# A two-bank split, a shared last eviction and halved activation stores at the end of a fused attention and expert kernel

## The chip, the cores and the metric

The kernel runs on one core of a Trainium2 chip. The metric is device time in microseconds (us), one launch for the whole computation. Below, PE is the matrix engine, DVE the vector engine, ACT the scalar engine, POOL the GpSimd engine and SP the engine that issues nearly all transfers. ACTq and SPq are the instruction queues of ACT and SP, in which transfers are issued, semaphores awaited and branches taken.

## The reference

The inputs are q, k and v of shape (8 batches, 8 heads, 576 tokens, 64). Attention goes through 32 landmarks per head: `A = sm(q, k_lm)`, `Bm = sm(q_lm, k_lm)`, `C = sm(q_lm, k)`, where a landmark is the mean of 18 consecutive tokens, and `sm` is a softmax of the scaled products. `Z` is an approximate inverse of `Bm` after six steps of `Z = 2 Z - Z Bm Z`, and the output of attention is `A Z C v`, reshaped to 4608 rows of 512.

Each row is then given to one of eight experts, the one whose embedding has the largest cosine with it, and the result is

```
h = np.maximum(x[mask] @ w1[e], 0.0)
out[mask] = gate_w[mask, None] * (h @ w2[e])
```

with `w1[e]` 512 x 1024 and `w2[e]` 1024 x 512; the gate is the chosen expert's softmax probability. The output is 4608 x 512 in float32.

## The kernel before, in words

The kernel guesses one expert per batch from the batch's first results, runs all 576 rows of the batch through that expert, and counts the rows for which the guess was wrong. Only if that count is above zero does a general path run behind it: `general(...)` stands under `tc.If(left[0] > 0)` on L1590, and its code lies between that branch and the end of the program. With the given data the count is zero, so every engine branches over it, then waits at L1590 and L1630 for all work and ends.

Products are made in float16 with split operands: each operand is a high and a low part, and three products (high by high, high by low, low by high) are summed in PSUM. PSUM is one tile `ps` of eight banks of 512 float32 columns, and `take` hands out banks by number.

The instruction order is written out by hand. `Weave` runs generators, one for each piece of work, and the string `TURNS` says which generator goes next; `CHOICES` says which engine does a piece that either could do, and `BANKS` which bank a request gets. Each engine executes its instructions in the order in which they come out. The tile framework adds the semaphores: an instruction waits for the earlier ones that touch the same tile, and for `ps` the same bank. A transfer's issue may also be held until an older transfer has landed whose semaphore it reuses.

The pieces that the change touches:

- `held` (L957): the activations `ab[b]` of a batch, 128 partitions x 2 parts (high, low) x 2 x 576 in float16, are stored to DRAM (`abs_`, L967) for the general path, one transfer of 576 KB per batch on SP. There are three `ab` buffers for eight batches.
- `second` (L1478): the second product of a batch. For each group of 128 rows (`c` = 0 to 3; `c` = 4 is a group of 64 rows) eight weight pieces are multiplied into one bank `py`, three matmuls each. The very last group (batch 7, `c` = 3) is made in two halves of 256 columns: first all eight pieces for columns 0 to 255, then all eight for columns 256 to 511, both in the one bank of `py`. The matmuls are recorded on the helper's line L505.
- `outputs` (L1517): a finished group is multiplied by its gate factor on its way from PSUM to the SBUF tile `yt`, by DVE (L1533) or ACT (L1535), and stored by SP (L1540; the 64-row group by L1543). The last half goes to ACT alone, which also issues its store:

```
last = (b, c, cols.stop) == (B - 1, 3, DM)
...
(act if last else sp).dma_start(out[t0:t0 + P, cols], yt[:, 0:n])
```

Ahead of the eviction of the last group's first half, `values_load` (L1523) reads the count of wrong guesses into a register of every engine.

Two lines of `rows`, which the change leaves alone, matter to the prediction: on L1194 DVE sums the router columns (64 onward) of each half bank and on L1197 ACT squares the first 64 columns, so the two read different columns of the same banks, and write to different tiles.

Of the kernel before, what the change touches and what calls it, by code (L numbers as in the profile page):

```python
# [13 lines left out]
AF = mybir.ActivationFunctionType  # L14
ALU = mybir.AluOpType
# [4 lines left out]
P = 128  # L20
B, H, S, D = 8, 8, 576, 64
# [8 lines left out]
DM = H * D  # L30
# [115 lines left out]
def T(ns, n, lat=None, cols=None, tiles="whole"):  # L146

    return "use", "pe", ns, lat, (2.3 * ns if cols is None else cols, n), tiles
# [319 lines left out]
def nystrom_moe(ctx: ExitStack, tc: tile.TileContext, qT, kT, v, emb, w1, w2, out):  # L468
    nc = tc.nc
    vec, act, pool, pe, sp = nc.vector, nc.scalar, nc.gpsimd, nc.tensor, nc.sync  # L470
# [12 lines left out]
    def view(ids):  # L483

        return ps[:, ids[0]] if len(ids) == 1 else ps[:, ids[0]:ids[0] + len(ids)]

    def take(work, n, *shares):

        shares = shares or ("att",)
        if work:  # L490
            ids = yield (*work, n, shares)
        else:
            for x in shares:
                yield "get", x, None, n
            ids = yield "get", "bank", None, n

        def done():
            wv.put("bank", *ids)
            for x in shares:
                wv.put(x, *ids)  # L500

        return view(ids), done

    def mm(o, lhsT, rhs, start=True, stop=True):
        pe.matmul(o, lhsT, rhs, start=start, stop=stop)  # L505
# [74 lines left out]
    abs_ = dram.tile([B, P, 2, 2, S], F16, name="abs_")  # L580
    wgs_ = dram.tile([NU, P, 4, 2, WC], F16, name="wgs_")

    wv = Weave(bank=NBANKS - 1, att=99, quad=QUAD, ph=99, py=99, pv=99, half=1, **BUFS)
# [37 lines left out]
    qt, kt, vt, ab, abr, u0, x0, sums_of, rcs = {}, {}, {}, {}, {}, {}, {}, {}, {}  # L621
# [335 lines left out]
    def held(b):  # L957

        if b:
            yield "wait", ("ab", b - 1)  # L960
        i, = yield "get", "ab"
        abr[b] = abt[i]
        ab[b] = abt[i][:, PAD:PAD + 4 * S].rearrange("p (x g s) -> p x g s", x=2, g=2)
        wv.flag(("ab", b))
        yield "wait", ("rows", b)
        yield "use", "dma", TAKES["ab"], ISSUE["ab"]
        sp.dma_start(abs_[b], ab[b])  # L967
        yield "wait", ("first", b)
        wv.put("ab", i)

# [301 lines left out]
    def batch(b):  # L1272
        if b:
            yield "wait", ("begun", b - 1)
        yield "get", "land"
        yield "get", "u"
        u0[b] = wk.tile([P, 2, D], F32, name="u", bufs=BUFS["u"])
        wv.flag(("begun", b))
        if b < EARLY:
            wv.add(guess(b))  # L1280
        wv.add(held(b))
        wv.add(values(b))
        wv.add(queries(b))
        wv.add(landmarks(b))
        for cs in ROWS[b % 2]:
            wv.add(rows(b, cs))
        wv.add(route(b))
# [190 lines left out]
    def second(b):  # L1478

        if b:  # L1480
            yield "wait", ("y", b - 1, 4)

        order = (0, 1, 2, 3, 4) if b < B - 1 else (4, 0, 1, 2, 3)
        for c in order:
            py, done = yield from take(None, 1, "py")
            o = 64 * (b % 2) + P * c
            if c == 4:
                o = 0 if b % 2 else 512

            parts = 2 if (b, c) == (B - 1, order[-1]) else 1  # L1490
            n = DM // parts
            for f, x0 in [(f, n * i) for i in range(parts) for f in range(8)]:
                q = f // 2
                yield "wait", ("h", b, f)
                yield "wait", ("w2", b, q)
                ht = hts[b, f]
                w = w2c[b, q][:, :, DM * (f % 2):DM * (f % 2) + DM]
                yield T(648 / parts if c < 4 else 325, 6 if c < 4 else 12, 0.0, cols=3 * n if c < 4 else 3 * DM // 2,
                        tiles="whole" if c < 4 else "halves")
                for i, x in ((0, 0), (0, 1), (1, 0)):  # L1500
                    st_, sp_ = f == i == x == 0, f == 7 and i == 1
                    if c < 4:
                        mm(py[:, x0:x0 + n], ht[:, i, o:o + P], w[:, x, x0:x0 + n], start=st_, stop=sp_)
                    else:
                        for s in range(2):
                            mm(py[64 * s:64 * s + 64, 0:256], ht[:, i, o:o + 64], w[:, x, 256 * s:256 * s + 256],
                               start=st_, stop=sp_)
                if c == order[-1] and x0 + n == DM:
                    wv.put("ht")
                    if f % 2 == 1:  # L1510
                        wv.put("w2")
                if parts == 2 and f == 7 and x0 == 0:
                    wv.add(outputs(b, c, py, None, S * b + o, slice(0, n)))
            wv.flag(("y", b, c))
            wv.add(outputs(b, c, py, done, S * b + o, slice(DM - n, DM)))

    def outputs(b, c, py, done, t0, cols):  # L1517
        yield "sleep", LAT["pe"]
        yield "wait", ("gfac", b)
        if (b, c, cols.start) == (B - 1, 3, 0):  # L1520

            yield "wait", "mi"
            left.append(nc.values_load(mi[0:1, 0:1], min_val=0, max_val=NT))  # L1523
        yield "get", "yt"
        n = cols.stop - cols.start if c < 4 else DM // 2
        if c == 4:
            cols = slice(0, n)
        fac = gfac[:, b, c:c + 1]
        last = (b, c, cols.stop) == (B - 1, 3, DM)
        who = yield "any", (("act", n / 1.2 + 145), ("dve", (n + 66) / 0.96 + 57))[:1 if last else 2]  # L1530
        yt = wst.tile([P, DM], F32, name="yt", bufs=BUFS["yt"])
        if who == "dve":
            vec.tensor_scalar(yt[:, 0:n], py[:, cols], fac, None, op0=ALU.mult)  # L1533
        else:
            act.activation(yt[:, 0:n], py[:, cols], AF.Copy, scale=fac)  # L1535
        if done:
            done()
        yield "use", "dma", TAKES["out"], ISSUE["out"]
        if c < 4:
            (act if last else sp).dma_start(out[t0:t0 + P, cols], yt[:, 0:n])  # L1540
        else:
            for s in range(2):
                sp.dma_start(out[t0:t0 + 64, 256 * s:256 * s + 256], yt[64 * s:64 * s + 64, 0:256])  # L1543
        yield "sleep", 2000.0
        wv.put("yt")
# [36 lines left out]
    for b in range(B):  # L1582

        wv.add(first(b))
        wv.add(second(b))
# [47 lines left out]
```

## Time and profile before

| | us |
|---|---|
| median of three runs | 412.91 (412.23 to 415.27) |
| the profiled execution | 412.15 |
| its span, first to last instruction | 410.3 |

The profiled execution lies 0.76 us below the median, and 1.85 us of it lie outside the span. In the page's table of busy time PE has 394.3 us (96% of the span), DVE 327.8 (80%), ACT 245.8 (60%) and POOL 78.2 (19%). The 16 transfer engines moved 77.68 MB, 189 GB/s on average. The granted clock of TensorE is 0.992 on average over the span. To read such a table: busy shares say which engine could be the limit over the whole span, not what happens in its last ten microseconds, where the change mostly lies; for that the single instructions have to be read in order of time.

### The profile page before, as it was taken

The numbers are of one execution on the slowest core, as the hardware profiler recorded it, in microseconds if no ns is written. First come the engines' busy times: TensorE is split into PE (matmuls) and PEld (weight loads), VectorE is DVE, ScalarE is ACT, GpSimd is POOL, SyncE is SP. The second block draws the span as 40 slices with busy tenths as digits, with TensorE's granted clock in tenths as the row PEclk, the third lists the DMA queues.
The fourth block names the chain that finished last, engine by engine and source line by source line (L and its number), as shares of the span: only waits on it lengthen the run. The fifth ranks groups of instructions, "written<-read, shape, count | busy, mean of one in ns | idle before, by whom it ended". The sixth has DMA issues, their size and how long they took to land.

```text
span 410.3 us, 14583 instructions
## 1 busy us (share of the span) xinstructions
PE 394.3 (96%) x6079; PEld 243.7 (59%) x6079; DVE 327.8 (80%) x996; ACT 245.8 (60%) x547; POOL 78.2 (19%) x82
## 2 busy tenths in 40 slices
PE   7889999999999999999999999999999999999995
PEld 3455744677655774557755575457755585457644
DVE  5879989888888997977979888886997598588431
ACT  1368877676577575663768577544557867535300
POOL 5051246201222132102132232001211203000100
PEclk9969999999999999999999999999999999999999
DMA  8879793733598089425694189022283119232102
GB/s 305 335 251 354 279 329 141 251 102 119 184 375 309 12 291 385 181 68 201 207 375 184 51 260 365 27 69 84 90 278 148 62 48 332 104 138 77 77 27 98
DMA packets 23947, 77.68 MB, mean 189 GB/s; under 512 B 3009, under 2 KB 6337, under 8 KB 22081
## 3 DMA queue, kind: packets, MB, share of 16 engines
q1 hardware_dynamic: 23584, 76.49, 51.8%
q8 instruction: 49, 0.80, 0.8%
q10 hardware_dynamic: 288, 0.18, 0.2%
q14 instruction: 26, 0.20, 0.2%
HBM read 61.92 MB, written 14.75 MB: 187 GB/s over the span
## 4 chain that ended last, share of the span: by engine, by line
PE 60%; DMA 18%; DVE 11%; ACT 6%; issue 3%; POOL 1%; SPq 0%; ACTq 0%; DVEq 0%; POOLq 0%
PE ps L505 58%; DMA wstage<-w 8%; DMA q_t<-qT 6%; DMA k_t<-kT 4%; DVE ht L1444 2%; DVE w2c L1434 2%; POOL half L668 1%; ACT junk L1405 1%; ACT junk L1326 1%; ACT ec L821 1%; PE ps L869 1%; ACT w2c L1432 1%; DVE cm L813 1%; ACT ht L1442 1%; ACT ae L929 0%
## 5 line engine op out<-in xcount | busy, mean ns | idle before, releaser
L505 PE MATMUL ps<-w2c,ht 128*128 128x512 f16 (+2 forms) x1176 | 197.8, 340 | 1.2 <-issue 0.6
L505 PEld LDWEIGHTS <-ht 128*128 128x128 f16 (+1 forms) x1176 | 94.8, 102 | 82.1 <-issue 4.0
L505 PE MATMUL ps<-ab,ww 128*128 128x288 f16 x768 | 100.7, 286 | 0.9 <-DVE ht L1444 0.9
L505 PEld LDWEIGHTS <-ww 128*128 128x128 f16 x768 | 73.8, 98 | 24.5 <-issue 3.3
L1442 ACT ACTIVATE ht<-ps 128x288 f16<-128x288 f32 x128 | 47.9, 412 | 36.5 <-PE ps L505 36.2
L1444 DVE SCALAR_TENSOR_TENSOR ht<-ps,ht 128x288 f16<-128x288 f32 x128 | 52.3, 447 | 5.1 <-ACT ht L1442 5.1
L1434 DVE SCALAR_TENSOR_TENSOR w2c<-wstage,wsc,w2c 128x1024 f16<-128x1024 f32 x32 | 42.6, 1330 | 1.0 <-ACT w2c L1432 0.9
L1326 ACT ACTIVATE junk<-wstage 128x1024 bf16<-128x1024 f32 x32 | 33.8, 1056 | 7.3 <-DMA wstage<-w 6.8
L1197 ACT ACTIVATE junk<-ps 128x512 bf16<-128x512 f32 (+1 forms) x40 | 23.8, 594 | 22.1 <-DVE lg L1194 21.4
L1535 ACT ACTIVATE yt<-ps,gfac 128x512 f32<-128x512 f32 (+1 forms) x25 | 15.5, 619 | 23.7 <-PE ps L505 13.9
L1405 ACT ACTIVATE junk<-wstage 128x1024 bf16<-128x1024 f32 x26 | 27.4, 1055 | 2.1 <-DMA wstage<-w 1.8
L953 POOL TENSOR_TENSOR ae<-ae,am 128x576 f32<-128x576 f32 x14 | 16.1, 1156 | 64.4 <-DVE am L926 61.0
L668 POOL TENSOR_TENSOR half<-q_t 128x576 f32<-128x576 f32 x13 | 18.4, 1417 | 49.3 <-DMA q_t<-qT 23.0
L1215 POOL TENSOR_TENSOR nrm<-ssq,half 128x5 f32<-128x5 f32 x8 | 9.5, 1186 | 87.8 <-ACT junk L1197 87.8
L953 POOL TENSOR_TENSOR ae<-ae,asum 128x576 f32<-128x576 f32 x13 | 16.0, 1232 | 52.8 <-DVE asum L782 18.7
L668 POOL TENSOR_TENSOR half<-k_t 128x576 f32<-128x576 f32 x11 | 14.3, 1299 | 55.4 <-DMA k_t<-kT 38.3
L1432 ACT ACTIVATE w2c<-wstage,wsc 128x1024 f16<-128x1024 f32 x21 | 23.9, 1148 | 0.0
L1389 ACT ACTIVATE ww<-ps,wsc 128x1024 f16<-128x1024 f32 (+1 forms) x18 | 17.6, 1017 | 8.9 <-DVE wsc L1339 7.6
L1391 DVE SCALAR_TENSOR_TENSOR ww<-ps,wsc,ww 128x1024 f16<-128x1024 f32 (+1 forms) x18 | 20.7, 1156 | 2.1 <-ACT ww L1389 2.0
L505 PE MATMUL ps<-ek 32*32 32x64 f32 (+1 forms) x768 | 17.1, 221 | 3.6 <-DVE ek L1012 3.6
L505 PEld LDWEIGHTS ps<-ek 32*32 32x32 f32 x768 | 12.2, 108 | 12.0 <-DVE ek L1012 6.3
L821 ACT ACTIVATE ec<-ps,cneg 128x576 f32<-128x576 f32 x16 | 11.8, 736 | 10.3 <-DVE cneg L815 8.3
(214 smaller groups left out, 515.8 us busy)
## 6 DMA issues: line engine op xcount, KB each, us to landing
wstage<-w SPq DMA_DIRECT2D x64, 512.0 KB, 6.8
v<-v SPq DMA_DIRECT2D x16, 512.0 KB, 5.3
k_t<-kT SPq DMA_DIRECT2D x7, 1152.0 KB, 9.8
q_t<-qT SPq DMA_DIRECT2D x7, 1152.0 KB, 8.0
out<-yt SPq DMA_DIRECT2D x31, 256.0 KB, 4.0
abs__137<-ab SPq DMA_DIRECT2D x8, 576.0 KB, 4.7
k_t<-kT SPq DMA_DIRECT2D x2, 576.0 KB, 4.6
q_t<-qT SPq DMA_DIRECT2D x2, 576.0 KB, 6.6
```

The lines of the kernel that those rows point to most:

```text
L505: pe.matmul(o, lhsT, rhs, start=start, stop=stop)
L668: pool.tensor_tensor(out=half, in0=sv[:, :, :, 0:9], in1=sv[:, :, :, 9:18], op=ALU.add)
L953: pool.tensor_tensor(out=x, in0=x, in1=z, op=op)
L1197: act.activation(junk[lo:hi, 0:512].rearrange("p (j g x) -> p j g x", j=4, g=2), pfv[lo:hi, :, n, :, 0:D], AF.Square, accum_out=ssq[lo:hi, ...
L1326: act.activation(junk, stage[1, b, q], AF.Square, accum_out=sq[:, q:q + 1])
L1389: act.activation(ww[:, 0], pw, AF.Copy, scale=sc)
L1391: vec.scalar_tensor_tensor(out=ww[:, 1], in0=pw, scalar=sc, in1=ww[:, 0], op0=ALU.mult, op1=ALU.subtract)
L1405: act.activation(junk, stage[2, b, q], AF.Abs, accum_out=sq[:, q:q + 1])
L1432: act.activation(w[:, 0], st, AF.Copy, scale=sc)
L1434: vec.scalar_tensor_tensor(out=w[:, 1], in0=st, scalar=sc, in1=w[:, 0], op0=ALU.mult, op1=ALU.subtract)
L1442: act.activation(ht[:, 0, r], ph[:, 0:HS], AF.Relu)
L1444: vec.scalar_tensor_tensor(out=ht[:, 1, r], in0=ph[:, 0:HS], scalar=0.0, in1=ht[:, 0, r], op0=ALU.max, op1=ALU.subtract)
```

## The change

The last group of rows takes two neighbouring banks instead of one, one for each half of the columns. The last half is evicted by ACT (its first 128 columns) and DVE (its last 128 columns), and stored as two transfers of 64 KB, one issued by ACT and one by SP. The stores of the activations of batches 5, 6 and 7 are issued as two transfers each, the high and the low part.

```diff
@@ held @@
-        sp.dma_start(abs_[b], ab[b])
+        if b < 5:
+            sp.dma_start(abs_[b], ab[b])
+        else:
+            for x in range(2):
+                sp.dma_start(abs_[b, :, x], ab[b][:, x])
@@ second @@
-            py, done = yield from take(None, 1, "py")
+            parts = 2 if (b, c) == (B - 1, order[-1]) else 1
+            py, done = yield from take(None, parts, "py")
...
-                        mm(py[:, x0:x0 + n], ht[:, i, o:o + P], w[:, x, x0:x0 + n], start=st_, stop=sp_)
+                        mm(py[:, x0:x0 + n] if parts == 1 else py[:, x0 // n, 0:n], ht[:, i, o:o + P], w[:, x, x0:x0 + n], start=st_, stop=sp_)
...
-                    wv.add(outputs(b, c, py, None, S * b + o, slice(0, n)))
+                    wv.add(outputs(b, c, py[:, 0], None, S * b + o, slice(0, n)))
             wv.flag(("y", b, c))
-            wv.add(outputs(b, c, py, done, S * b + o, slice(DM - n, DM)))
+            wv.add(outputs(b, c, py if parts == 1 else py[:, 1], done, S * b + o, slice(DM - n, DM)))
@@ outputs @@
-        if who == "dve":
-            vec.tensor_scalar(yt[:, 0:n], py[:, cols], fac, None, op0=ALU.mult)
+        if last:
+            act.activation(yt[:, 0:n // 2], py[:, 0:n // 2], AF.Copy, scale=fac)
+            vec.tensor_scalar(yt[:, n // 2:n], py[:, n // 2:n], fac, None, op0=ALU.mult)
+        elif who == "dve":
+            vec.tensor_scalar(yt[:, 0:n], py[:, 0:n], fac, None, op0=ALU.mult)
         else:
-            act.activation(yt[:, 0:n], py[:, cols], AF.Copy, scale=fac)
+            act.activation(yt[:, 0:n], py[:, 0:n], AF.Copy, scale=fac)
...
-        if c < 4:
-            (act if last else sp).dma_start(out[t0:t0 + P, cols], yt[:, 0:n])
+        if last:
+            for e, h in ((act, 0), (sp, n // 2)):
+                e.dma_start(out[t0:t0 + P, cols.start + h:cols.start + h + n // 2], yt[:, h:h + n // 2])
+        elif c < 4:
+            sp.dma_start(out[t0:t0 + P, cols], yt[:, 0:n])
```

## Rows read from the trace of the kernel before

**Rows 1.** The page: busy time (share of the span) and instructions of each engine.

```profile
PE 394.3 (96%) x6079; PEld 243.7 (59%) x6079; DVE 327.8 (80%) x996; ACT 245.8 (60%) x547; POOL 78.2 (19%) x82
```

**Rows 2.** The chain that ended last, from 395 us on: start, us, what.

```profile
394.97 7.62 PE ps L505 x48
402.59 0.02 issue
402.62 0.50 DVE yt L1533
403.11 0.04 issue
403.15 2.79 PE ps L505 x24
405.95 0.03 ACTq L1535
405.98 0.05 issue
406.02 0.47 ACT yt L1535
```

**Rows 3.** The timeline from 400 us: start, us, engine, line, operation, [idle before, its releaser].

```profile
401.52 1.94 SPq L1540 DMA_DIRECT2D out<-yt  x2
402.62 0.48 DVE L1533 TENSOR_SCALAR yt<-ps,gfac 128x256 f32<-128x256 f32 x1 [1.12 <-PE ps L505]
406.53 0.36 ACTq L1540 DMA_DIRECT2D out<-yt  x1
```

**Rows 4.** Line L1590, the branch: durations ns min/median/max, first and last start us.

```profile
L1590 SPq EVENT_SEMAPHORE  x9: 17/17/17, 407.3 to 408.6; - x9
L1590 POOLq EVENT_SEMAPHORE  x5: 17/43/43, 399.6 to 400.0; - x5
L1590 POOLq COMPARE_BRANCH  x1: 45/45/45, 397.1 to 397.1; - x1
L1590 DVEq COMPARE_BRANCH  x1: 72/72/72, 402.6 to 402.6; - x1
L1590 PEldq COMPARE_BRANCH  x1: 3778/3778/3778, 403.8 to 403.8; - x1
L1590 SPq COMPARE_BRANCH  x1: 53/53/53, 403.8 to 403.8; - x1
L1590 DVEq EVENT_SEMAPHORE  x1: 21/21/21, 405.5 to 405.5; - x1
L1590 ACTq COMPARE_BRANCH  x1: 54/54/54, 406.9 to 406.9; - x1
L1590 ACTq EVENT_SEMAPHORE  x1: 17/17/17, 407.4 to 407.4; - x1
```

**Rows 5.** Waits of SP's queue from 395 us: total us, times, longest.

```profile
SPq L1590 <- SPq L1590: 4.2, 2, 3.5
```

**Rows 6.** Line L1630, the end of the program, SP alone.

```profile
L1630 SPq EVENT_SEMAPHORE  x14: 17/28/28, 408.6 to 410.3; - x14
```

**Rows 7.** Line L1540 of SP from 400 us; transfers from 395 us: count, KB each, us to landing.

```profile
L1540 SPq DMA_DIRECT2D out<-yt x2: 338/338/338, 401.5 to 403.1; - x2
...
out<-yt SPq DMA_DIRECT2D x1, 128.0 KB, 2.0
out<-yt ACTq DMA_DIRECT2D x1, 128.0 KB, 1.8
```

**Rows 8.** Evictions by shape, whole span: count | busy us, mean ns | idle before.

```profile
L1535 ACT ACTIVATE yt<-ps,gfac 128x512 f32<-128x512 f32 x17 | 11.6, 685 | 4.1 <-PE ps L505 1.8 <-DVE gfac L1265 1.2 <-issue 1.1
L1533 DVE TENSOR_SCALAR yt<-ps,gfac 128x512 f32<-128x512 f32 x14 | 10.3, 742 | 2.9 <-DMA out<-yt 2.2 <-DVE gfac L1269 0.4 <-PE ps L505 0.3
```

**Rows 9.** The timelines of ACT and DVE around 385 us.

```profile
385.16 0.19 ACT L1197 ACTIVATION_READ_ACCUMULATOR junk<-ps 128x1 f32 x1
385.65 0.60 ACT L1197 ACTIVATE junk<-ps 128x512 bf16<-128x512 f32 x1 [0.29 <-DVE lg L1194]
...
385.39 0.22 DVE L1194 TENSOR_REDUCE lg<-ps 128x8 f32<-128x64 f32 x1 [0.81 <-ACT junk L1197]
```

**Rows 10.** The timeline of SP from 350 to 380 us; its longest wait from 395 us.

```profile
360.59 0.45 SPq L967 DMA_DIRECT2D abs__137<-ab  x1
367.56 1.21 SPq L967 DMA_DIRECT2D abs__137<-ab  x1
378.30 0.58 SPq L967 DMA_DIRECT2D abs__137<-ab  x1
...
SPq L1523 <- DVE gfac L1269: 17.4, 1, 17.4
```

More of the change, by code (lines that the diff above doesn't have):

```diff
@@ L1488, in second @@
                 o = 0 if b % 2 else 512
-            parts = 2 if (b, c) == (B - 1, order[-1]) else 1
             n = DM // parts
```

## The prediction

> **What bounds the kernel now.** The busy shares come first: PE works 96% of the span [rows 1], so the body is PE's, and nothing in the change alters PE's work there. What is left is the tail, so I read the chain that ended last, from 395 us on. There PE finishes the first half of the last rows at 402.59 us, waits, and starts the second half at 403.15; between the two stands DVE's eviction of the first half [rows 2, 3]. The wait is 0.56 us, on an eviction that reads other columns than PE is about to write. PE ends at 405.94 (403.15 + 2.79), ACT evicts from 406.02 for 0.47 and issues the store at 406.53; it lands 1.8 us later, at 408.3 [rows 2, 3, 7].
>
> The chain of waits stops at ACT's eviction; the span ends only at 410.3. For the rest I read the branch's line and the end's [rows 4 to 6]. The reader should see three things there. First, the branch itself takes about 50 ns on SP, DVE, POOL and ACT, but the first instruction behind it starts much later: on SP 3.5 us after (403.8 to 407.3), on DVE 2.9 (402.6 to 405.5), on POOL 2.5 (397.1 to 399.6), on ACT only 0.5 (406.9 to 407.4); PE's branch itself lasts 3.8 us. The branch jumps over the code of the general path. Second, SP is the engine that then waits for every transfer: nine semaphores from 407.3 to 408.6, with one real wait among them, 4.2 - 3.5 = 0.7 us, for ACT's store; the nine without it take 0.6. Third, SP's end takes 1.7 us more (408.6 to 410.3). So SP's jump was made while PE and ACT still worked, and had only 0.7 us to spare. **The last work of SP sets when its jump begins**, and before the change that work was the first half's store, issued at 403.1 [rows 7].
>
> **The change, part by part.**
>
> Two banks: PE's 0.56 us wait goes, since DVE now reads a bank that PE doesn't write. The second half starts at 402.59 and ends at 405.38. DVE's eviction of the first half then runs beside PE and nobody waits for it but its store on SP, which is issued at 403.1 as before. Gain on PE's end: 0.56.
>
> The last eviction: ACT takes 685 ns for 512 columns and 474 for 256 [rows 2, 8], so 106 ns for 128 columns and 368 for an eviction of 128. DVE takes 742 and 484 [rows 3, 8], so 129 and 355. Whether they run side by side is the question. Around 385 us ACT and DVE read different columns of the same banks and write to different tiles, and they strictly alternate: ACT ends at 385.35, DVE starts at 385.39; DVE ends at 385.61, ACT starts at 385.65; each is booked as waiting for the other [rows 9]. The new pair reads two column ranges of one bank, so I take it as serial, ACT first, with 0.04 us between. With the 0.08 us that ACT took to start after PE [rows 2]: ACT 405.46 to 405.83, DVE 405.87 to 406.22. The bounds: side by side, DVE would end at 405.82, 0.40 earlier; no row allows worse than serial. The split thus gains nothing over ACT alone: 368 + 40 + 355 = 0.76 us against 0.47.
>
> The last store: ACT's part is issued about 405.87 and is out of the way. SP's part is issued 0.02 us after DVE ends, as at 403.1, so at 406.24, and lands 1.8 to 2.0 us later by the two 128 KB rows [rows 7]; I charge 64 KB at no less, for want of a nearer row: 408.2.
>
> SP's jump, the step that decides: SP can't branch before it has issued its part. From the start of its last issue to its branch SP took 0.7 us (403.1 to 403.8); ACT took 0.4 for the same pair (406.5 to 406.9) [rows 3, 4, 7]. I take SP's own: branch at 406.94. Then 3.5 us by SP's own row, with 2.5 (POOL) and 3.8 (PE) as the ends: 410.44. Then the nine semaphores without any real wait, 0.6, since both stores landed two microseconds before, and the end, 1.7: **the span ends at 412.7 instead of 410.3, 2.4 us later**. With the short ends (0.4, 2.5 and side-by-side evictions) it is 405.84 + 0.4 + 2.5 + 2.3 = 411.0, 0.7 later; with PE's 3.8 it is 413.0, 2.7 later.
>
> DVE's jump moves too: its branch comes with its last eviction (402.6 in both rows), so now near 405.9, and its first instruction behind at 408.8; SP's 410.4 covers it by 1.6 us. ACT's branch moves ahead by about 0.7 and isn't late. PE's moves ahead with its half.
>
> The activation stores: three issues more on SP. Those in place last 0.45, 1.21 and 0.58 us [rows 10], so a second one costs at most 1.2 each. Behind the first SP next issues at 367.2, behind the second at 377.1, and behind the third one store and then a wait of 17.4 us at L1523 until 396.5 [rows 10]. These idle stretches hide all three. No one on this path reads the stored activations, and the buffers of batches 5 to 7 are not filled again. The bytes are the same. If a held issue were to use up that cover it would still have the 17.4 us. Cost 0, on either side, and no place for a gain.
>
> The sum: the profiled execution was 412.15 us, its span 410.3; +2.4 gives 414.55. It lies 0.76 below the median of the three runs, and on that scale the sum is 415.3. I put the number between, nearer to the profile, as two of the four executions seen lie at 412.2: **414.8**.
>
> **The rivals.** A: the jump costs nothing (or SP's code is there in time, as ACT's nearly was: 0.5 us). Then SP's semaphores wait for its own store's landing, 408.05 to 408.25, and from a landing to the end it takes 2.0 us as before (408.3 to 410.3): 410.05 to 410.25, 0.05 to 0.25 earlier, or up to 0.65 with side-by-side evictions. Time 411.5 to 412.1, on the median's scale up to 412.9: the change as one would read it from the chain of waits. For it speaks that the branches last 50 ns and that ACT's jump was short; against it, three engines out of five needed 2.5 to 3.5 us until their next instruction, and SP itself 3.5. The Trainium skill, "Advanced Engine Details and Errata", Control Flow Timing, gives a compare-and-branch about 108 ns; by that alone this rival's time would follow. The rows agree on the branch, not on what comes behind it.
>
> B, on the slow side by more than the forecast: SP's jump queues behind DVE's. DVE's branch at 405.9 lies 1.0 ahead of SP's; if SP's code came only after DVE's had, SP would wait the 2.9 - 1.0 = 1.9 us that DVE's has left before its own 3.5 begin: 4.3 us later than before, 416.5, on the median's scale 417.2, just over 1%. It decides from a gap of 5.2 us between SP's branch and its next instruction on. Against it: before, DVE's branch lay 1.2 ahead of SP's and PE's came with SP's, and SP's 3.5 us already hold whatever that crowding costs.
>
> C: the two evictions overlap and the jump costs as forecast: 0.40 less, 414.15. Rows 9 speak against it.
>
> **How the numbers follow.** Forecast (jump exposed, 2.5 to 3.8 us, serial evictions) 0.78, C 0.05, A 0.12, B 0.05. The forecast with its bounds and both scales spans 413.2 to 415.6; with the spread of a few tenths between executions, and taking in half of A's upper end, the range is 412.3 to 416.4. Differences under 1% (4.1 us) can't be told from no change on this kernel. A's and the forecast's times all lie within that, B's just beyond; faster by 1% has no mechanism here: 0.01, same 0.93, slower 0.06.
>
> **What would show it.** Right: PE's second half starts without a gap near 402.6 and the wait on DVE's eviction is gone; DVE's last eviction starts as ACT's ends; SP's branch stands near 406.9, its next instruction at 409.5 to 410.7, and no semaphore of SP at L1590 waits after it. Wrong: SP's first instruction behind the branch within 1 us (A), or more than 5 us later (B); ACT's and DVE's last evictions starting together (C); any stretch before 395 us that is longer or shorter than before, which the sum rules out.

## The result, and the profile after

The changed kernel takes 415.73 us (median of 22 runs, 413.15 to 417.98) against 412.92 (22 runs, 410.52 to 416.28): a ratio of 1.0051, 95% interval 1.0032 to 1.007, so 1.3 to 2.9 us slower. The ratio is the one on record for undisturbed runs; the two medians lie 2.8 us apart, at the upper end of its interval. Its profiled execution has a span of 413.6 us against 410.3.

The chain of waits of the kernel after, from 395 us on (start, us, what), answers to [rows 2]:

```profile
394.86 12.19 PE ps L505 x81
407.05 0.03 ACTq L1537
407.07 0.04 issue
407.12 0.38 ACT yt L1537
407.50 0.03 issue
407.52 0.35 DVE yt L1538
```

PE now runs through: one piece to 407.05, with no eviction in it. From the start of DVE's eviction of the first half to PE's end it was 3.32 us before (402.62 to 405.94) and is now 2.60 (404.45, in the next fence, to 407.05): 0.72 less: the 0.56 of the wait and 0.16 more, which is what the restart costs. A matmul of this shape lasts 0.27 us (the line below, of the kernel before), but 24 of them take only 2.79, so one starts about every 0.11 us and overlaps the one ahead by 0.16; behind a gap that overlap is lost. Then ACT and DVE follow each other.

```profile
L505 PE MATMUL ps<-w2c,ht 128*128 128x256 f16 x48 | 5.6, 272 | 0.6 <-DVE yt L1533 0.6
```

The timeline after, from 404 us (columns as in [rows 3]):

```profile
404.45 0.48 DVE L1540 TENSOR_SCALAR yt<-ps,gfac 128x256 f32<-128x256 f32 x1 [1.15 <-PE ps L505]
404.96 0.34 SPq L1550 DMA_DIRECT2D out<-yt  x1
407.12 0.37 ACT L1537 ACTIVATE yt<-ps,gfac 128x128 f32<-128x128 f32 x1 [7.67 <-PE ps L505]
407.52 0.36 ACTq L1548 DMA_DIRECT2D out<-yt  x1
407.52 0.35 DVE L1538 TENSOR_SCALAR yt<-ps,gfac 128x128 f32<-128x128 f32 x1 [2.59 <-ACT yt L1537]
407.90 0.33 SPq L1548 DMA_DIRECT2D out<-yt  x1
```

The releaser in brackets says it: DVE's part waited for ACT's, and SP's last issue comes at 407.90. DVE's wait is for a semaphore that the program has ACT raise; the two parts share a bank and the tile `yt`. Whether the chip would have let them run side by side without it, no run shows.

The branch's line after (now L1600), the waits of SP's queue and the end's line (now L1640), answering to [rows 4 to 6]:

```profile
L1600 SPq EVENT_SEMAPHORE  x9: 17/17/17, 411.4 to 412.0; - x9
...
L1600 PEldq COMPARE_BRANCH  x1: 4158/4158/4158, 404.9 to 404.9; - x1
L1600 DVEq COMPARE_BRANCH  x1: 72/72/72, 407.5 to 407.5; - x1
L1600 ACTq COMPARE_BRANCH  x1: 54/54/54, 407.9 to 407.9; - x1
L1600 SPq COMPARE_BRANCH  x1: 53/53/53, 408.3 to 408.3; - x1
L1600 ACTq EVENT_SEMAPHORE  x1: 17/17/17, 408.4 to 408.4; - x1
...
L1600 DVEq EVENT_SEMAPHORE  x1: 21/21/21, 410.5 to 410.5; - x1
```

```profile
SPq L1600 <- SPq L1600: 3.0, 1, 3.0
```

```profile
L1640 SPq EVENT_SEMAPHORE  x14: 17/28/28, 412.0 to 413.6; - x14
```

SP branches at 408.3, has its next instruction at 411.4, and then runs through nine semaphores without a stop (0.6 us; one wait instead of two) and the end (1.6). The jump stands openly at the end of the path. DVE and SP jump side by side, 3.0 and 3.1 us.

To compare kernels whose bodies differ by chance, the **tail** is used below: from the start of the cast of the wrong-guess count, the same instruction in all of them, to the end of the span. Before and after:

```profile
396.32 0.15 DVE L1561 CAST misi<-misf 128x1 int32<-128x1 f32 x1
```

```profile
398.16 0.15 DVE L1571 CAST misi<-misf 128x1 int32<-128x1 f32 x1
```

410.3 - 396.32 = 14.0 us before, 413.6 - 398.16 = 15.4 after: **the tail grew by 1.4 us**. The other 1.8 us between the two profiles lie ahead of the cast, and 1.7 of them ahead of the first instruction that differs (the first split store, at 362.42), as the same DVE instruction shows in the two timelines near 347 us:

```profile
346.97 0.13 DVE L1251 RECIPROCAL nrm<-nrm 128x5 f32<-128x5 f32 x1
```

```profile
348.68 0.13 DVE L1255 RECIPROCAL nrm<-nrm 128x5 f32<-128x5 f32 x1
```

SP's timeline after, the stores of the activations (L971), answering to [rows 10]:

```profile
362.42 0.95 SPq L971 DMA_DIRECT2D abs__137<-ab  x2
369.00 0.34 SPq L1550 DMA_DIRECT2D out<-yt  x1
369.38 1.55 SPq L971 DMA_DIRECT2D abs__137<-ab  x2
378.98 1.11 SPq L1553 DMA_DIRECT2D out<-yt  x2
380.14 1.08 SPq L971 DMA_DIRECT2D abs__137<-ab  x2
381.26 1.48 SPq L1550 DMA_DIRECT2D out<-yt  x1
```

The first two pairs end several us before SP's next work. The third stands, with one store behind it, in front of the long wait at L1527, which takes it up (15.8 us instead of 17.4).

### The profile page after: what moved, and what is told of

Same layout as the page of the kernel before. It is cut to its first block, busy times and chain, and to the rows that moved or that the text cites. A ratio compares the mean times of both kernels' runs of the same rounds, so it can differ in the third digit from the quotient of the medians.

```text
span 413.6 us, 14591 instructions
## 1 busy us (share of the span) xinstructions
PE 396.0 (96%) x6079; PEld 242.7 (59%) x6079; DVE 328.7 (79%) x997; ACT 246.4 (60%) x547; POOL 78.2 (19%) x82
## 4 chain that ended last, share of the span: by engine, by line
PE 60%; DVE 16%; DMA 13%; ACT 5%; issue 3%; POOL 1%; SPq 1%; DVEq 0%; ACTq 0%; POOLq 0%
PE ps L505 58%; DMA wstage<-w 8%; DMA q_t<-qT 3%; DVE ht L1448 3%; DVE w2c L1438 2%; DMA k_t<-kT 1%; DVE cm L813 1%; POOL half L668 1%; ACT ec L821 1%; PE ps L869 1%; ACT w2c L1436 1%; PE ps L591 1%; DVE ksum L671 1%; ACT junk L1409 1%; ACT ht L1446 1%
## 5 line engine op out<-in xcount | busy, mean ns | idle before, releaser
L668 POOL TENSOR_TENSOR half<-k_t 128x576 f32<-128x576 f32 x11 | 14.3, 1300 | 58.9 <-DMA k_t<-kT 39.4
L1542 ACT ACTIVATE yt<-ps,gfac 128x512 f32<-128x512 f32 (+1 forms) x24 | 15.0, 625 | 15.4 <-DVE gfac L1273 7.5
L1198 DVE TENSOR_REDUCE lg<-ps 128x8 f32<-128x64 f32 (+1 forms) x40 | 8.9, 222 | 11.7 <-ACT junk L1201 5.9
```

Of the source, the lines that this page charges most:

```text
L668: pool.tensor_tensor(out=half, in0=sv[:, :, :, 0:9], in1=sv[:, :, :, 9:18], op=ALU.add)
```

## The experiments

The theory: what costs is SP's jump, which begins only after SP's last issue and has nothing beside it. Rival A: the jump is free, as in the prediction's A; the tail must then have grown by the serial evictions, the smaller stores or the added issues. Rival B: SP's jump queues behind DVE's. All tails and gaps come from one profile each; ratios are to the kernel before. The diffs are against the changed kernel, but for e5, e8 and e9, which are edits of the kernel before.

| kernel | tail us | SP's branch to next instruction us | ratio (95% interval) |
|---|---|---|---|
| before | 14.0 | 3.5 | |
| after | 15.4 | 3.1 | 1.0051 (1.0032 to 1.007) |
| after, again (e12) | 15.4 | 2.9 | 1.0038 (1.0008 to 1.0068) |
| e1 two banks alone | 13.5 | 3.2 | 0.998 (0.9951 to 1.001) |
| e2 two banks, split activation stores | 13.4 | 2.8 | 0.9962 (0.9935 to 0.999) |
| e2 again (e11) | 14.3 | 2.7 | 0.9993 (0.997 to 1.0016) |
| e7 as e2, first half's store on ACT | 13.7 | 2.9 | 0.9988 (0.9955 to 1.002) |
| e3 after, both last stores on ACT | 14.1 | 2.7 | 0.9984 (0.9948 to 1.0019) |
| e10 after, last issues swapped | 15.0 | 2.9 | 1.0036 (1.0008 to 1.0064) |
| e4 after, activation stores whole | 15.6 | 3.2 | 1.0013 (0.9977 to 1.005) |
| e5 before, last store on SP | 15.6 | 2.7 | 1.0011 (0.9974 to 1.0047) |
| e5 again (e8) | 15.5 | 2.6 | one run |
| e6 after, general path cut | 12.2 | 0.2 | 0.9946 (0.9909 to 0.9983) |
| e9 before, general path cut | 13.1 | 0.2 | 1.0001 (0.9965 to 1.0037) |

**The last store on SP, nothing else (e5, and e8 once more).**

```diff
-            (act if last else sp).dma_start(out[t0:t0 + P, cols], yt[:, 0:n])
+            sp.dma_start(out[t0:t0 + P, cols], yt[:, 0:n])
```

> The kernel before with one edit: the last store is issued by SP instead of ACT. Theory: SP issues it 10.2 us into the tail, branches 0.4 to 0.7 later, has its next instruction 3.1 to 3.5 us after that and ends 2.3 us on: tail 16.0 to 16.7 us, 2.0 to 2.7 more than before. Rival A (no cost in the jump): 14.0 to 14.2 us, a landing 0.2 later at most. Rival B (SP's code waits for another engine's): above 17.5.

> A second look at e5, the kernel before with its last store on SP, for the spread of SP's jump: theory 3.1 to 3.5 us from the branch to the next instruction, tail 16.0 to 16.7 us, as in e5.

The branch's line of e5, SP and the end of DVE's jump, and its cast:

```profile
L1590 SPq EVENT_SEMAPHORE  x9: 17/17/17, 410.6 to 411.2; - x9
...
L1590 DVEq EVENT_SEMAPHORE  x1: 21/21/21, 406.7 to 406.7; - x1
...
L1590 SPq COMPARE_BRANCH  x1: 53/53/53, 407.9 to 407.9; - x1
```

```profile
397.31 0.15 DVE L1561 CAST misi<-misf 128x1 int32<-128x1 f32 x1
```

The span is 412.9, the tail 15.6: 1.6 us more than before by that one edit. The mechanism is there and A is not, but the size is under the 16.0 expected: the gap was 2.7 (2.6 in the second profile, tail 15.5) instead of 3.1 to 3.5, and the branch came 0.4 after the issue, not up to 0.7. B is not there either: DVE was through its jump at 406.7, 1.2 us before SP's branch, and SP's still took 2.7. In time e5 can't be told from the kernel before; its interval ends at 1.9 us more, so it takes in the 1.6 of the tail.

**The changed kernel with both last stores on ACT (e3).**

```diff
-            for e, h in ((act, 0), (sp, n // 2)):
+            for e, h in ((act, 0), (act, n // 2)):
```

> The changed kernel with one edit: ACT issues both parts of the last store. Theory: SP's last issue is then the first half's store, 2.9 us earlier, its jump lies beside the last eviction and the landing, and the last store lands 1.8 us after 9.8 us: tail 13.3 to 13.4 us, 2.1 less than the changed kernel's 15.4, though the two evictions still follow one another. Rival A (the jump costs nothing; the tail grew by the serial evictions, the smaller stores or the extra issues): 15.4, as the changed kernel.

The branch's line of e3 (SP), SP's waits, and the transfers from 403 us (count, KB each, us to landing):

```profile
L1600 SPq EVENT_SEMAPHORE  x9: 17/17/17, 408.9 to 411.4; - x9
...
L1600 SPq COMPARE_BRANCH  x1: 53/53/53, 406.2 to 406.2; - x1
```

```profile
SPq L1600 <- SPq L1600: 4.7, 3, 2.7
```

```profile
out<-yt SPq DMA_DIRECT2D x1, 128.0 KB, 3.4
out<-yt ACTq DMA_DIRECT2D x2, 64.0 KB, 2.7
```

SP's jump lies at 406.2 to 408.9, beside the last eviction, and 1.3 of the 1.4 us are gone (14.1). But the tail missed 13.3 to 13.4: SP then waited 4.7 - 2.7 = 2.0 us for the stores, which took 2.7 us to land where I had put 1.8. The times go the same way: e3's interval ends at 1.0019, the changed kernel's begins at 1.0032 (that of its repeat, e12, at 1.0008).

**SP's last issue 0.38 us earlier (e10).**

```diff
-            for e, h in ((act, 0), (sp, n // 2)):
+            for e, h in ((sp, 0), (act, n // 2)):
```

> The changed kernel with the two last issues swapped: SP stores the part that ACT evicts first, ACT the part that DVE evicts after it. SP's last issue comes 0.38 us earlier, 9.36 us into the tail instead of 9.74. Theory: SP's branch and its end move with it, 0.4 less for the same gap: tail 14.6 to 15.5 us by a gap of 2.6 to 3.5, 15.1 with the 3.1 of the changed kernel. Rival (the end is set by the last landing or by DVE's jump): 15.4 or more whatever SP's gap is.

15.0, within what was expected: the issue came 0.38 earlier and the gap was 2.9. The step is no larger than the spread of the gaps, so alone it would show little; it stands with e3 and e5.

**The jump over next to no code (e6, and its counterpart e9).** Both cut the body of the general path, which doesn't run with this data.

```diff
         dram = ctx.enter_context(tc.tile_pool(name="gdram", bufs=1, space=DRAM))
+
+        upper = one.tile([P, P], BF16, name="upper")
+        pool.memset(upper, 1.0)
+        return
 
         def mm(o, lhsT, rhs, start=True, stop=True):
```

> The changed kernel with the body of the general path, which never runs with this data, cut to one memset: the branch is taken as before, over next to no code. Theory (what costs is that the target's code has to be brought in): SP's next instruction comes within 0.5 us of its branch, as ACT's does, and the tail ends with the landing of SP's store: 13.3 to 13.6 us, about 2 less than the changed kernel's 15.4. Rival (a taken branch at the end costs SP 3 us wherever it goes): 15.4.

> The kernel before with the body of the general path, which never runs with this data, cut to one memset, as in e6. It is e6's counterpart without the change. Theory: with no code to bring in, SP waits for ACT's store, issued 10.2 us into the tail and landing 1.6 to 1.8 later, and the end takes 0.8 us as in e6: tail 12.6 to 12.9 us, against 12.2 in e6; then the change's two banks do pay once the jump is free. Rival (the change's pieces are slower in themselves): 12.2 us or less.

The branch's line of e6 (SP), its end's line, and the transfers from 404 us:

```profile
L1604 SPq COMPARE_BRANCH  x1: 53/53/53, 410.4 to 410.4; - x1
```

```profile
L1644 SPq EVENT_SEMAPHORE  x9: 17/28/28, 410.6 to 412.4; - x9
```

```profile
q14 instruction: 2, 0.02, 0.6%
...
out<-yt SPq DMA_DIRECT2D x1, 128.0 KB, 1.7
out<-yt ACTq DMA_DIRECT2D x1, 64.0 KB, 1.6
```

The same branch, 53 ns, and 0.2 us later SP goes on: the 3 us belong to the code behind the branch, not to branching. The packets of instructions, the transfers that bring the engines their code, say the same: from SP's branch to the end of the span seven are moved after the change, none in e6. The tail is 12.2, over a us under the expected 13.3 to 13.6. The cut also removed fourteen of the twenty-three semaphores on SP's two lines behind the branch (9 and 14; nine are left), at 0.07 us each an estimated 0.9 us, and the stores landed in 1.6. e9 came out at 13.1, just above its 12.6 to 12.9.

Between the two, with the jump free in both, **the tail of the change is 0.9 us shorter than that of the kernel before**. Half of it, 0.45, is the issue of the last store, 9.75 us into the tail instead of 10.20: the two banks give 0.72, and the two evictions in a row take 0.28 of that back (0.75 us against 0.47 for ACT alone). The other half lies behind the issue, 0.2 of it in the landing (1.6 and 1.8). So the change as a whole gains once the jump is free, though its shared eviction loses, and the jump turns the gain into a loss. This rests on one profile each, both without code that the kernel needs; in time the intervals of e6 and e9 overlap.

**Two banks alone (e1), with the split activation stores (e2, e11), and the first half's store on ACT too (e7).**

```diff
         if last:
-            act.activation(yt[:, 0:n // 2], py[:, 0:n // 2], AF.Copy, scale=fac)
-            vec.tensor_scalar(yt[:, n // 2:n], py[:, n // 2:n], fac, None, op0=ALU.mult)
+            act.activation(yt[:, 0:n], py[:, 0:n], AF.Copy, scale=fac)
...
-            for e, h in ((act, 0), (sp, n // 2)):
-                e.dma_start(out[t0:t0 + P, cols.start + h:cols.start + h + n // 2], yt[:, h:h + n // 2])
+            act.dma_start(out[t0:t0 + P, cols], yt[:, 0:n])
```

(e1 has `if b < 8` in `held`, so that all activation stores are whole; e7 also gives the last group's first store to `act`.)

> The kernel before with the last rows' halves in two banks and nothing else: one eviction of 256 columns on ACT, its store of 128 KB issued by ACT, the activation stores whole. Its tail is read from the start of the cast of the wrong-guess count on DVE to the end of the span: 14.0 us before, 15.4 us after the change. Theory (SP's jump is the cost): PE ends 0.7 earlier, ACT evicts and stores as before, SP's jump lies beside that work, so the tail is 13.3 us, 0.7 less than before. Rival 1 (the two banks gain nothing, something else is late at once): 14.0. Rival 2 (the slower tail comes from the two banks themselves): above 14.0.

> As e1, with the activation stores of batches 5 to 7 in two transfers each. Theory: the three extra issues cost nothing and only change which of SP's eight transfer semaphores the last store ends on, so that three of the four semaphores of 0.07 us behind it are waited for before it lands: tail 13.1 us, 0.2 less than e1. Rival (the extra issues hold something up): above e1's 13.3.

> e2 once more (two banks, one eviction and the last store on ACT, activation stores in two transfers), for its time beside the changed kernel on one chip. Theory: tail 13.1 to 13.4 us as in e2, about 2 less than the changed kernel, so a time about 0.5% below it and 0.1 to 0.2% below the kernel before. Rival: no difference from the changed kernel beyond the intervals.

> As e2 (two banks, one eviction on ACT, activation stores in two transfers), with the first half's store also issued by ACT, so that SP's last issue is the store of the group before. Theory: SP's jump is hidden already in e2 by about 0.5 us and is now hidden by 2; the tail stays at 13.1 us. Rival (the jump still binds in e2, where it begins 7.2 us into the tail and takes up to 3.5): e2 is 0.1 to 0.4 us longer than this one.

The transfers of e2 and of e11, the same kernel, from 403 us:

```profile
out<-yt SPq DMA_DIRECT2D x1, 128.0 KB, 3.8
out<-yt ACTq DMA_DIRECT2D x1, 128.0 KB, 2.1
```

```profile
out<-yt SPq DMA_DIRECT2D x1, 128.0 KB, 4.0
out<-yt ACTq DMA_DIRECT2D x1, 128.0 KB, 3.0
```

e1 came out at 13.5, nearer to its 13.3 than to the rivals' 14.0 and more; e2 (13.4) and e7 (13.7) missed their 13.1. e2 and e11 are one kernel with tails of 13.4 and 14.3: the 0.9 between them is the landing of the last store, 2.1 and 3.0 us. I had expected 13.1 to 13.4. The tails of e1, e2 and e7 are 0.3 to 0.6 us shorter than before, e11's is 0.3 longer. Of these four only e2's interval lies below 1, and the repeat doesn't bear it out: two banks without the shared eviction are the best version found that keeps the general path, below the changed kernel where both ran on one chip (0.9993 against 1.0038, with intervals that overlap by 0.0008), and not shown to be faster than the kernel before. e7 is no shorter than e2, but landings scatter by more than the 0.1 to 0.4 us in question. SP's waits in e2 settle it:

```profile
SPq L1598 <- SPq L1598: 4.0, 3, 2.8
```

Behind its jump of 2.8 us SP waited 1.2 us more for stores, so the jump didn't bind there.

**The activation stores whole again (e4), and the changed kernel once more (e12).**

```diff
-        if b < 5:
+        if b < 8:
             sp.dma_start(abs_[b], ab[b])
```

> The changed kernel with the activation stores whole again. Theory: SP's jump ends after all transfers have landed, so neither the extra issues nor the semaphore on which the last store ends matter: tail 15.4 us, as the changed kernel. Rival (the extra issues are part of the cost): 0.4 us or more below that.

> The changed kernel itself once more beside e11. Theory: tail 15.0 to 15.9 us by SP's gap of 2.6 to 3.5; time 0.3 to 0.5% above the kernel before. Rival: no slower than the kernel before.

15.6 and 15.4: the extra issues are no part of the cost of the tail. Nor do they slow the body: the stretch that holds them, from the reciprocal near 347 us to the cast, takes 49.0 to 49.5 us in the eight profiles with split stores and in the six with whole ones alike. The cast itself stood between 396.3 and 400.3 over all profiles, and at 398.16 and 396.74 in the two of the changed kernel. So the 1.8 us ahead of the cast in the profile after are not the activation stores'; why the stretch ahead of them varies stays open. In time e4's interval (0.9977 to 1.005) takes in the changed kernel's ratio as well as 1 and decides nothing.

## Why the prediction was right, point by point

**The direction and the place held**, and the change stayed under 1%; the time lies in the range, 0.9 us above the number. By terms:

- PE's end: 0.56 was charged, 0.72 came. PE's restart costs 0.16 too, which the row of the wait doesn't hold.
- The evictions: serial as forecast (C is out), 368 and 351 ns on L1537 and L1538, against 368 and 355.
- From SP's last issue to its branch: 0.4 us (407.9 to 408.3), not the 0.7 taken from SP's one row; the low end was the right one, in every kernel in which SP issued the last store. The 0.7 is no scatter: it came again in e1 and e9. What makes it there stays open.
- The jump: 3.1 us, not 3.5; over the kernels with the full general path 2.6 to 3.5. The row that I took was the longest of them.
- The nine semaphores and the end: 2.2, against 2.3. No store was waited for.
- The sum: +2.4 was forecast for the tail, +1.4 came: 0.3 from the branch, 0.4 from the jump, 0.2 from PE and 0.1 from the end. The mechanism was right and the size too large by these. That the time came so near the number is in part luck and doesn't bear out the size: the ratio of 1.0051 is 2.1 us, of which the tail of the profiles shows 1.4 (the repeat e12 has 1.6 in time and 1.4 in the tail). By the tail alone, 412.92 + 1.4, it would have been 0.5 below the number. The rest lies within the interval, and whether any of it belongs to the change stays open.
- The signs: SP's branch and its next instruction came at 408.3 and 411.4; less the 1.8 us by which this profile's body is longer, that is 406.5 and 409.6, near the 406.9 and within the 409.5 to 410.7 of the forecast. One sign of being wrong did show, a stretch before 395 us longer than before. It was badly chosen: two profiles of the changed kernel differ there by 1.4, and the stretch that holds the split stores didn't grow.
- That differences under 1% can't be told from no change was too strict: with 22 runs of each the interval, 1.0032 to 1.007, leaves out 1.
- A is out: the same branch costs 0.2 us over short code and 3.1 over the general path. The Trainium skill, "Runtime: NRT & Kernel Launch", Instruction fetch mechanics, says that a taken branch to code that is not yet at hand has to wait for its fetch. These runs agree: 3.1 us with seven packets of instructions moved, 0.2 with none. The Trainium skill, "Advanced Engine Details and Errata", Control Flow Timing, gives a compare-and-branch about 108 ns. The rows do not agree with that on the branch itself, though the prediction says so: it took 45 to 72 ns on SP, DVE, ACT and POOL. What costs here is what follows it. ACT's jump stayed at 0.5 us wherever the general path was in place, and why is not shown; in the source of that path ACT has one line.
- B is out: DVE's jump (407.5 to 410.5) and SP's (408.3 to 411.4) overlap, and in e5 SP's took 2.7 us with DVE's long over.
- The activation stores at 0: e4 and e12 agree.

What I had not weighed is how a store lands while code is fetched. The prediction didn't depend on it, since SP's jump outlasted every landing, but the expectations of e1, e2, e3 and e11, with 1.8 us for the last landing, did.

## What to carry to other kernels

Read on past the last computing instruction: find for each engine when its last work ends and what it still has to do before the program can end, above all the engine that closes it. Give the last store to an engine whose way to the end is short (here ACT, 0.5 us from its branch to its next instruction), and let the closing engine begin its way early: here the one queue that must not issue last is SP's. Before splitting an eviction over two engines, look for what keeps the halves apart: here, in one bank and one tile, they only queued. Whether two banks would have let them overlap was not tried.

## What the runs showed of the hardware that was not expected

A store lands late when a part of it stands behind a packet of instructions. In the kernel after, the transfers from 404 us:

```profile
q8 instruction: 2, 0.03, 2.0%
q14 instruction: 6, 0.05, 1.6%
...
out<-yt SPq DMA_DIRECT2D x1, 128.0 KB, 3.9
out<-yt ACTq DMA_DIRECT2D x1, 64.0 KB, 2.5
out<-yt SPq DMA_DIRECT2D x1, 64.0 KB, 2.3
```

The first half's 128 KB took 3.9 us here and 1.7 in e6, where no engine had far to jump (two packets of instructions instead of eight); the 64 KB parts 2.3 to 2.5 and 1.6. What the 3.9 us are can be read from the packets themselves. The store has 144 of them, which is nine to each of the 16 transfer engines if they are spread evenly. From 405.7 to 406.4 us 135 are moved, and one packet of instructions begins (queue: packets, MB, share of 16 engines):

```profile
q1 hardware_dynamic: 135, 0.12, 50.2%
q8 instruction: 1, 0.02, 15.1%
```

Then none is moved until 407.6. From 407.60 to 408.37:

```profile
q1 hardware_dynamic: 9, 0.01, 6.7%
```

In the trace the packet of instructions runs from 405.93 to 407.63, and the nine begin at 407.61. It is so in all nine profiles of kernels with two banks and the general path: the first half's store took 3.2 to 4.0 us, and its last nine packets began within 0.02 us of the end of that one packet. That the nine share a transfer engine with it is inferred from these counts.

Fetching alone doesn't make a store late. In the kernel before the same packet began at 404.87, when all 144 had been moved (403.9 to 404.8), and the store took 2.0 us:

```profile
q1 hardware_dynamic: 144, 0.13, 43.1%
```

The packet follows PE's branch by 1.0 to 1.9 us. Before, that branch came 0.7 us behind the issue of the first half's store; with two banks PE no longer waits and branches at the same moment. The late landing is thus an effect of the change that the prediction didn't have. It cost nothing in the changed kernel, where SP's jump ends later. A store's size said little: 64 KB landed hardly sooner than 128 KB under the same conditions (1.6 and 1.7 in e6).
